# Spreading the maxima of k over the partitions: a transpose of the broadcast column in place of a float32 matrix product

## The chip, the core and the metric

The kernel runs on one core of a Trainium2 chip. Its time is device microseconds (us) of one launch; the clock starts and ends outside the span that the profiler shows, so a run's time is a little longer than its span. Five engines work side by side, each through its own queue in order: PE (TensorE; its weight loads are listed as PEld), ACT (ScalarE), DVE (VectorE), POOL (GpSimd, all but unused here) and SP (SyncE, which issues the transfers). An instruction waits at the head of its engine's queue until the semaphores that it names are there, and all that stands behind it on that engine waits too.

## The reference

Softmax attention without a sequence-by-sequence product, then two two-layer networks over the 4608 rows.

```python
def _attn_ref(q, k, v):                       # (8, 8, 576, 64): batch, heads, sequence, head width
    q_s = np.exp(q - np.max(q, axis=-1, keepdims=True))
    q_s = q_s / (np.sum(q_s, axis=-1, keepdims=True) + 1e-09)
    k_s = np.exp(k - np.max(k, axis=2, keepdims=True))      # maximum over the sequence
    k_s = k_s / (np.sum(k_s, axis=2, keepdims=True) + 1e-09)
    kv = np.einsum('bhsd,bhse->bhde', k_s, v)
    return np.einsum('bhsd,bhde->bhse', q_s, kv)

def _moe_ref(x, w_in, w_out):                 # 512 -> 2048 -> 512
    r = np.maximum(x @ w_in, 0.0)
    return (r * r) @ w_out

def _moe2_ref(x, w_gate, w_val, w_out):       # 512 -> 1536 -> 512
    gate = 1.0 / (1.0 + np.exp(-(x @ w_gate)))
    return (gate * (x @ w_val)) @ w_out
```

The change is in the third line of the attention: the maximum of k over the sequence, one number for each of the 64 columns of a head, has to be taken from every row of k, and rows lie on partitions.

## The kernel before, in words

Float32 products are made of three products of a high and a low part (`mm3`, L219 to L221), which is nearly all that PE does. The 4608 rows are nine blocks j of 512. Blocks 0 to 2 go through the first network by plain products (`c_in` and `c_out`; their middle results are `g0hl`); the later blocks go in pairs through seven products of half-size matrices instead of eight (`PRODUCTS`; their operands are `bX` for the first layer and `bS` for the second). Weights are split once and written to device memory; later they come back by `w_fetch` (L320) as tiles `ws`. Banks `bank0` to `bank5` of PSUM take the sums. At the end of block 2, `c_ev` copies `bank0` to `bank3` out: ACT copies two (L213, `x<-bank`), DVE the two others (L942, `x<-bank`), and SP stores the four (L947).

Attention for later blocks runs in the gaps. For a batch b and a pair of head pairs p (16 times in all) `plan_k` lays down this chain:

- DVE: `k_max` (L461, L464), the maximum of the sequence pieces, `kmx`;
- PE: `k_turn` (L470), two transposes of `kmx` into the PSUM tile `kps` (for b = 0 into a bank);
- DVE: `k_col` (L475), the maximum along the free axis, a column `km` of one number for each partition;
- PE: `k_all` (L483), which spreads that column over all partitions; this is what changes;
- DVE: `k_sub` (L488), k minus its maxima; ACT: `k_exp` (L492); PE: `k_mm` (L504), the products with v; DVE: `k_rec` (L512, L513); ACT: `k_copy` (L522).

For a block j and a pair p `plan_q` lays down a similar one: for j from 2 on DVE reduces (L565), PE swaps halves (`q_swap`, L575), DVE subtracts (L585, L586), ACT takes exp (L590), DVE sums (L565), PE swaps again (L575), DVE divides (L604 to L615) and transposes (L621), and PE multiplies by kv (L641).

The order of all of this isn't written out by hand. `Plan` holds each step with a due time, the cost that it is thought to have on its engine, the steps that it comes after and the buffers that it takes and gives. `Plan.trace` plays the steps through with these costs and records each when the engine comes free in that play:

```python
                    fn(*[e if a is CHOSEN else a for a in args])
                    us = engines[e]
                    busy[e] = now + us
```

So a cost in the table doesn't only describe a step: it decides what stands before what on every queue. The steps of the k chain touched here stand in `plan_k` (L666); the step of `k_all` is named "kgm" and has the cost 0.46 (1.1 for b = 0) on PE.

Of the kernel before, what the change touches and what calls it, by code (L numbers as in the profile page):

```python
# [23 lines left out]
DMA, PE, ACT, DVE, POOL, FREE = "DMA PE ACT DVE POOL FREE".split()  # L24
# [5 lines left out]
class Plan:  # L30
# [13 lines left out]
    def add(self, key, engines, name, fn, *args, after=(), take=(), give=(), slack=0.0):  # L44
        n = len(self.ops)
        assert name not in self.names, name
        self.names[name] = n
        self.ops.append((key, n, engines, name, fn, args, tuple(after), tuple(take), tuple(give), slack))
# [94 lines left out]
def attention_mlp_mlp(  # L143
# [20 lines left out]
    nc = tc.nc  # L164
# [24 lines left out]
    ident = cst.tile([128, 128], F32, name="ident")  # L189
# [6 lines left out]
    add = plan.add  # L196
# [281 lines left out]
    def k_all(b, p):  # L478

        m1, ps = kmx.pop((b, p)), kps[b, p]  # L480
        for n in range(2):
            at = slice(2 * C + C * n, 3 * C + C * n)
            nc.tensor.matmul(ps[:, at], m1[:, n:n + 1].to_broadcast([128, 128]), ident, start=True, stop=True)  # L483

    def k_sub(b, p):
        kt = kt_t[b, p].rearrange("p n (r c) -> p n r c", c=C)
# [177 lines left out]
    slack = lambda j: SLACK if j > 4 else 0.0  # L664

    def plan_k(b, p, key, step, wait=()):  # L666
        n = (b, p)
        vs = [(b, 2 * p + x) for x in range(2)]
        bank = [] if b == 0 else ["pa"]
        if b:  # L670
            add(key - 5, {DMA: 3.7}, ("kt",) + n, kv_load, b, p, after=wait, take=["k", "k"])
        else:
            add(p, {DMA: 1.84}, ("kt",) + n, k_load, b, p, take=["k"])
        for x in vs:
            if not b:
                add(p + 4, {DMA: 1.15}, ("vt",) + x, v_load, *x, take=["W"])
            add(key + 2.5 * step, {ACT: 0.22}, ("vo",) + x, v_ones, *x, after=[("kt",) + n if b else ("vt",) + x])
        for r in range(RK - 1):
            add(
                key + 0.1 * r, {DVE: 0.35}, ("km",) + n + (r,), k_max, b, p, r,  # L680
                after=[("km",) + n + (r - 1,) if r else ("kt",) + n], take=[] if r else ["km"],
            )
        add(key + 0.5 * step, {PE: 0.25 if b else 0.6}, ("kt2",) + n, k_turn, b, p, after=[("km",) + n + (RK - 2,)], take=bank, slack=slack(b))
        add(key + step, {DVE: 0.35}, ("kdg",) + n, k_col, b, p, after=[("kt2",) + n])
        add(key + 1.5 * step, {PE: 0.46 if b else 1.1}, ("kgm",) + n, k_all, b, p, after=[("kdg",) + n], give=["km"], slack=slack(b))
        add(key + 2 * step, {DVE: 1.4}, ("ks",) + n, k_sub, b, p, after=[("kgm",) + n], give=bank)
        add(key + 3 * step, {ACT: 1.15}, ("ke",) + n, k_exp, b, p, after=[("ks",) + n])
        add(
            key + 4 * step, {PE: 1.22 if b else 2.3}, ("kp",) + n, k_mm, b, p, after=[("ke",) + n] + [("vo",) + x for x in vs],
            take=bank, give=["k"] + (["k"] if b else ["W", "W"]), slack=slack(b),  # L690
        )
        add(key + 5 * step, {DVE: 0.36}, ("kr",) + n, k_rec, b, p, after=[("kp",) + n], take=["kr"])
        add(
            key + 6 * step, {ACT: 1.3}, ("kv",) + n, k_copy, b, p,
            after=[("kr",) + n] + (kv_users[b - 2, p] or [("kv", b - 2, p)] if b > 1 else []), give=["kr"] + bank,
        )
# [348 lines left out]
    for p in range(NP // 2):  # L1045
        plan_k(0, p, 3.37 * p, 0.86)
        plan_q(0, p, 3.37 * p + 3.62, 0.41)
# [67 lines left out]
    def plan_blocks(js, t, per):  # L1115

        for j in js:
            new = [b for _, b in segs(j) if b not in done_b]
            done_b.update(new)
            for p in range(NP // 2):  # L1120
                for b in new:
                    plan_k(b, p, t, 0.82, x_before.get(j, []))
                plan_q(j, p, t + 3.26, 0.58)
                t += 2 * per / NP
# [363 lines left out]
```

## Time and profile before

| | us |
|---|---|
| median of 3 runs | 1609.53 (1608.44 to 1611.57) |
| the profiled execution | 1610.02 |
| its span | 1608.2 |
| PE busy | 1577.2, 98% of the span |
| DVE busy | 1226.5, 76% |
| ACT busy | 940.2, 58% |
| waits of PE from 112 us on | 0.9 |

The span is what the profiler shows from the first to the last instruction. PE is busy almost all of it; a matmul row's end is modelled, and neighbours overlap, so that the pace of PE is read from the starts of rows that follow each other, not from a row's duration. The page's view of transfers and its groups name tiles by the program's names: `kps` and `km` are the tiles of the k chain, `qsw` and `qst` those of the q chain, `whl` and `wf` weights that are being split, `ws` weights fetched back.

### The profile page before, as it was taken

The numbers are of one execution on the slowest core, as the hardware profiler recorded it, in microseconds if no ns is written. First come the engines' busy times: TensorE is split into PE (matmuls) and PEld (weight loads), VectorE is DVE, ScalarE is ACT, GpSimd is POOL, SyncE is SP. The second block draws the span as 40 slices with busy tenths as digits, with TensorE's granted clock in tenths as the row PEclk, the third lists the DMA queues.
The fourth block names the chain that finished last, engine by engine and source line by source line (L and its number), as shares of the span: only waits on it lengthen the run. The fifth ranks groups of instructions, "written<-read, shape, count | busy, mean of one in ns | idle before, by whom it ended". The sixth has DMA issues, their size and how long they took to land.

```text
span 1608.2 us, 23070 instructions
## 1 busy us (share of the span) xinstructions
PE 1577.2 (98%) x8028; PEld 1301.7 (81%) x8028; DVE 1226.5 (76%) x2105; ACT 940.2 (58%) x1711; POOL 0.7 (0%) x6
## 2 busy tenths in 40 slices
PE   5899999999999999999999999999999999999998
PEld 3678888788878878888888888888888888888898
DVE  8988785899989999987977796448834784458547
ACT  6877655668686958785854564335523552335344
POOL 0000000000000000000000000000000000000000
PEclk9999999999999999999999999999999999999999
DMA  8987999998999989899989998656875677555896
GB/s 278 303 311 262 352 344 349 354 322 338 344 350 314 334 289 337 290 356 295 316 278 377 314 335 253 217 191 229 268 235 195 208 233 245 191 195 192 252 406 237
DMA packets 206835, 462.03 MB, mean 287 GB/s; under 512 B 78976, under 2 KB 78976, under 8 KB 206720
## 3 DMA queue, kind: packets, MB, share of 16 engines
q1 hardware_dynamic: 206720, 460.56, 82.8%
q8 instruction: 64, 1.05, 0.3%
q14 instruction: 51, 0.42, 0.1%
HBM read 364.54 MB, written 95.94 MB: 286 GB/s over the span
## 4 chain that ended last, share of the span: by engine, by line
PE 93%; DMA 2%; DVE 2%; ACT 1%; SPq 1%; issue 0%; DVEq 0%; ACTq 0%
PE bank L219 30%; PE bank L220 30%; PE bank L221 30%; PE xps L641 1%; PE kps L504 1%; DMA wraw<-in_moe_w_in_dram 1%; DMA vt<-in_v_dram 0%; DMA kt<-in_k_dram 0%; DMA w_in<-whl 0%; DMA wraw<-in_moe_w_out_dram 0%; DVE whl L216 0%; PE kps L483 0%; DVE wf L297 0%; SPq L250 0%; PE qsw L575 0%
## 5 line engine op out<-in xcount | busy, mean ns | idle before, releaser
L219 PE MATMUL bank<-bX,ws 128*128 128x512 f32 (+1 forms) x1176 | 442.3, 376 | 0.1
L221 PE MATMUL bank<-bX,ws 128*128 128x512 f32 (+1 forms) x1176 | 440.0, 374 | 0.0
L220 PE MATMUL bank<-bX,ws 128*128 128x512 f32 (+1 forms) x1176 | 439.8, 374 | 0.0
L821 DVE TENSOR_TENSOR s<-s,bank 128x512 f32<-128x512 f32 (+1 forms) x315 | 202.9, 652 | 197.2 <-PE bank L221 169.1
L213 ACT ACTIVATE s<-bank 128x512 f32<-128x512 f32 (+1 forms) x315 | 178.1, 572 | 189.8 <-PE bank L221 185.5
L219 PE MATMUL bank<-bS,ws 128*128 128x512 f32 (+1 forms) x756 | 287.2, 380 | 0.7 <-ACT s L213 0.7
L220 PE MATMUL bank<-bS,ws 128*128 128x512 f32 (+1 forms) x756 | 285.4, 378 | 0.0
L221 PE MATMUL bank<-bS,ws 128*128 128x512 f32 (+1 forms) x756 | 285.3, 377 | 0.0
L213 ACT ACTIVATE bS<-s 128x512 fp32r<-128x512 f32 (+1 forms) x330 | 195.2, 601 | 118.7 <-PE bank L221 94.4
L219 PEld LDWEIGHTS bank<-bX,ws 128*128 128x128 f32 x1176 | 221.4, 188 | 41.3 <-issue 1.3
L221 PEld LDWEIGHTS bank<-bX,ws 128*128 128x128 f32 x1176 | 221.4, 188 | 39.7
L220 PEld LDWEIGHTS bank<-bX,ws 128*128 128x128 f32 x1176 | 221.5, 188 | 39.0
L216 DVE TENSOR_TENSOR bS<-s,bS 128x512 fp32r<-128x512 f32 (+1 forms) x330 | 211.1, 649 | 32.5 <-ACT bS L213 32.0
L219 PEld LDWEIGHTS bank<-bS,ws 128*128 128x128 f32 x756 | 142.3, 188 | 28.4 <-ACT s L213 1.5
L221 PEld LDWEIGHTS bank<-bS,ws 128*128 128x128 f32 x756 | 142.2, 188 | 26.4
L220 PEld LDWEIGHTS bank<-bS,ws 128*128 128x128 f32 x756 | 142.3, 188 | 25.9 <-DVE bS L216 0.4
L840 ACT ACTIVATE s<-s 128x512 f32<-128x512 f32 (+1 forms) x120 | 70.6, 589 | 154.0 <-DVE s L821 153.5
L760 DVE TENSOR_TENSOR s<-s,s 128x512 f32<-128x512 f32 (+1 forms) x192 | 122.0, 650 | 1.1
L216 DVE TENSOR_TENSOR whl<-wf,whl 128x512 fp32r<-128x512 f32 x127 | 85.8, 685 | 19.1 <-ACT whl L213 18.6
L213 ACT ACTIVATE whl<-wf 128x512 fp32r<-128x512 f32 x127 | 78.4, 625 | 34.1 <-DVE wf L311 11.5
L267 ACT ACTIVATE wf<-wraw 128x512 f32<-128x512 f32 x68 | 44.9, 663 | 29.2 <-DMA wraw<-in_moe_w_out_dram 24.3
L219 PE MATMUL bank<-x,whl 128*128 128x512 f32 x128 | 54.1, 423 | 4.8 <-ACT x L213 3.8
(115 smaller groups left out, 1896.3 us busy)
## 6 DMA issues: line engine op xcount, KB each, us to landing
ws<-w_out SPq DMA_DIRECT2D x221, 512.0 KB, 5.1
ws<-w_gv SPq DMA_DIRECT2D x210, 512.0 KB, 4.4
ws<-w_in SPq DMA_DIRECT2D x100, 512.0 KB, 5.8
w_out<-whl SPq DMA_DIRECT2D x53, 512.0 KB, 5.8
w_gv<-whl SPq DMA_DIRECT2D x42, 512.0 KB, 5.0
w_in<-whl SPq DMA_DIRECT2D x32, 512.0 KB, 6.1
kt<-in_k_dram SPq DMA_DIRECT2D x16, 640.0 KB, 6.2
x2r<-x SPq DMA_DIRECT2D x36, 256.0 KB, 5.0
```

What stands on the lines that cost most here:

```text
L213: nc.scalar.activation(out=dst, in_=src, func=AF.Copy)
L216: by_name[engine].tensor_tensor(out=dst, in0=src, in1=hi.bitcast(F32), op=ALU.subtract)
L219: nc.tensor.matmul(ps, ah, bh, start=first, stop=False, skip_group_check=True)
L220: nc.tensor.matmul(ps, ah, bl, start=False, stop=False, skip_group_check=True)
L221: nc.tensor.matmul(ps, al, bh, start=False, stop=last, skip_group_check=True)
L267: nc.scalar.activation(out=t, in_=high.bitcast(F32), func=AF.Abs)
L504: nc.tensor.matmul(ps[D * g:D * g + D, o:o + D + 1], kt[:, n, C * r + D * h:C * r + D * h + D], vt[:, c:c + D + 1], start=(r == 0), stop=( ...
L641: nc.tensor.matmul(ps[a][col:col + D, e], kvf[b % 2][2 * p + n][row], t[n][row, e], start=True, stop=True, skip_group_check=True)
L760: by_name[engine].tensor_tensor(out=t[o], in0=t[a], in1=t[b], op=ALU.subtract)
L821: nc.vector.tensor_tensor(out=t, in0=t, in1=banks[pr[b]][:, 0:n], op=ALU.add)
L840: nc.scalar.activation(out=t, in_=t, func=AF.Sigmoid)
```

## The change

`k_all` calls PE's transpose in place of a matrix product with the identity. Both have the broadcast column as one operand and the identity as the other, and both leave the same numbers in the same place. The cost of the step in the plan's table is lowered to that of `k_turn`.

```diff
@@ def k_all(b, p) @@
         for n in range(2):
             at = slice(2 * C + C * n, 3 * C + C * n)
-            nc.tensor.matmul(ps[:, at], m1[:, n:n + 1].to_broadcast([128, 128]), ident, start=True, stop=True)
+            nc.tensor.transpose(ps[:, at], m1[:, n:n + 1].to_broadcast([128, 128]), ident)
@@ def plan_k @@
-        add(key + 1.5 * step, {PE: 0.46 if b else 1.1}, ("kgm",) + n, k_all, b, p, after=[("kdg",) + n], give=["km"], slack=slack(b))
+        add(key + 1.5 * step, {PE: 0.25 if b else 0.6}, ("kgm",) + n, k_all, b, p, after=[("kdg",) + n], give=["km"], slack=slack(b))
```

The second line moves instructions on PE, DVE, ACT and SP in the first half of the program. The largest move is around the place where block 2 ends (the last `g0hl` products into `bank3`, number 1164 of PE's L219 to L221) and the first pair of later blocks begins.

PE, from the 11th `k_turn` of the program (batch 5, p = 0) to its `k_mm`, before. Lines of "..." stand for `mm3` products; the two L575 belong to two different q tiles:

```order
L470 MATMUL kps_3354<-ident_78,kmx_3260 128x128 x2
...
L483 MATMUL kps_3354<-ident_78,km1_3371 128x128 x2
...
L221 MATMUL bank3_92<-g0hl_3249,ws_3207 128x512
L575 MATMUL qsw_3404<-qst_3327,swap_80 128x32
L575 MATMUL qsw_3406<-qst_3374,swap_80 128x32
L219 MATMUL bank4_93<-bX_3143,ws_3376 128x512
...
L504 MATMUL kps_3457<-vt_3148,kt_3146 64x65 x20
```

PE at the same place now. The two L575 are the two swaps of one q tile (`qst_3348` and `qst_3400` are its maxima and its sums):

```order
L221 MATMUL bank3_92<-g0hl_3207,ws_3150 128x512
L575 MATMUL qsw_3368<-qst_3348,swap_80 128x32
L470 MATMUL kps_3380<-ident_78,kmx_3342 128x128 x2
L483 MATMUL kps_3380<-ident_78,km1_3389 128x128 x2
L575 MATMUL qsw_3411<-qst_3400,swap_80 128x32
L504 MATMUL kps_3424<-vt_3220,kt_3218 64x65 x20
L219 MATMUL bank0_89<-bX_3213,ws_3407 128x512
```

The 12 `mm3` products that stood between `k_turn` and `k_all`, and the 30 between `k_all` and `k_mm`, now stand elsewhere: the steps of one k chain and one q chain follow each other with nothing in between, ahead of the next stage's first product.

DVE at this place, before: `k_sub` (L488) stands ahead of the two copies out of the banks (L942).

```order
L475 TENSOR_REDUCE km1_3371<-kps_3354 128x2
L216 TENSOR_TENSOR whl_3351<-wf_3308,whl_3351 128x512
L565 TENSOR_REDUCE qst_3374<-qt_3287 128x32
L488 TENSOR_TENSOR kt_3146<-kt_3146,kps_3354 128x2x640
L277 TENSOR_SCALAR wf_3394<-wf_3394 128x512
L283 TENSOR_SCALAR wf_3394<-wf_3394 128x512
L290 SCALAR_TENSOR_TENSOR wf_3394<-wraw_3348,wf_3394 128x512
L942 COPY x2_3418<-bank1_90 128x512
L297 ISA wf_3394<-wraw_3348,wf_3394 128x1024
L942 COPY x2_3423<-bank3_92 128x512
```

DVE now, with the last of the copies first:

```order
L942 COPY x2_3378<-bank3_92 128x512
L585 TENSOR_TENSOR qst_3348<-qst_3348,qsw_3368 128x32
L586 TENSOR_TENSOR qt_3254<-qt_3254,qst_3348 128x1024
L475 TENSOR_REDUCE km1_3389<-kps_3380 128x2
L311 TENSOR_TENSOR wf_3081<-wf_3081,wf_3077 128x512
L216 TENSOR_TENSOR whl_3346<-wf_3189,whl_3346 128x512
L565 TENSOR_REDUCE qst_3400<-qt_3254 128x32
L488 TENSOR_TENSOR kt_3218<-kt_3218,kps_3380 128x2x640
```

The copies of the banks have moved ahead of the k chain's two DVE steps, and the subtraction of q, a weight's sum and split and the sum over q stand between them.

SP at this place, before: the fetches of the next stage's weights (L320) stand ahead of the stores of block 2 (L947).

```order
L257 DMA wraw_3348<-in_moe2_w_gate_dram 128x512
L320 DMA ws_3369<-w_in05_2521 128x1024
L320 DMA ws_3376<-w_in06_2603 128x1024
L320 DMA ws_3380<-w_in02_366 128x1024
L257 DMA wraw_3398<-in_moe2_w_val_dram 128x512
L315 DMA w_in37_3410<-whl_3315 128x1024
L320 DMA ws_3425<-w_in07_2566 128x1024
L947 DMA x2_2_0_3445<-x2_3408 128x512
```

SP now:

```order
L947 DMA x2_2_0_3385<-x2_3370 128x512
L947 DMA x2_2_1_3387<-x2_3372 128x512
L947 DMA x2_2_2_3393<-x2_3376 128x512
L947 DMA x2_2_3_3398<-x2_3378 128x512
L257 DMA wraw_3404<-in_moe2_w_gate_dram 128x512
L320 DMA ws_3407<-w_in05_2591 128x1024
L320 DMA ws_3414<-w_in06_2632 128x1024
```

The four stores, which wait for the copies, have moved ahead of the fetch of `ws_3407`, the weights of the first product behind L504 on PE.

## Rows read from the trace of the kernel before

**Rows 1.** The page: busy us, share of the span and instructions of each engine.

```profile
PE 1577.2 (98%) x8028; PEld 1301.7 (81%) x8028; DVE 1226.5 (76%) x2105; ACT 940.2 (58%) x1711; POOL 0.7 (0%) x6
```

**Rows 2.** Waits of PE after 112 us: total us, times, longest.

```profile
PE bank L219 <- ACT s L213: 0.7, 1, 0.7
PE kps L470 <- DVE kmx L464: 0.2, 1, 0.2
```

**Rows 3.** PE groups by form, later batches: busy us, mean ns, idle before.

```profile
L483 PE MATMUL kps<-ident,km 128*128 128x128 f32 x56 | 8.5, 274 | 0.0
L470 PE MATMUL kps<-ident,kmx 128*128 128x128 f32 x28 | 5.5, 278 | 2.0 <-DVE kmx L464 1.7 <-ACT qf L213 0.3
```

**Rows 4.** Timeline of PE, 131 to 136 us: start us, us, instructions.

```profile
131.86 0.39 PE L221 MATMUL bank<-x,whl 128*128 128x512 f32 x1
132.09 0.38 PE L470 MATMUL kps<-ident,kmx 128*128 128x128 f32 x2
...
132.54 0.39 PE L220 MATMUL bank<-x,whl 128*128 128x512 f32 x1
...
134.83 0.39 PE L221 MATMUL bank<-x,whl 128*128 128x512 f32 x1
135.06 0.61 PE L483 MATMUL kps<-ident,km 128*128 128x128 f32 x4
...
135.74 0.39 PE L220 MATMUL bank<-x,whl 128*128 128x512 f32 x1
```

**Rows 5.** Timeline of PE where block 2 ends, 340 to 350 us.

```profile
340.14 0.61 PE L483 MATMUL kps<-ident,km 128*128 128x128 f32 x4
...
343.11 0.39 PE L221 MATMUL bank<-g0hl,ws 128*128 128x512 f32 x1
343.34 0.53 PE L575 MATMUL qsw<-qst,swap 128*128 128x32 f32 x4
343.70 0.48 PE L219 MATMUL bank<-bX,ws 128*128 128x512 f32 x1
...
348.00 1.39 PE L504 MATMUL kps<-vt,kt 128*64 128x65 f32 x40
349.32 0.50 PE L219 MATMUL bank<-bX,ws 128*128 128x512 f32 x1
```

**Rows 6.** Timeline of DVE at the same place, 337 to 347 us.

```profile
337.94 0.42 DVE L475 TENSOR_REDUCE km<-kps 128x2 f32<-128x256 f32 x1
...
338.87 1.21 DVE L565 TENSOR_REDUCE qst<-qt 128x32 f32<-128x1024 f32 x1
340.78 1.49 DVE L488 TENSOR_TENSOR kt<-kt,kps 128x1280 f32<-128x1280 f32 x1 [0.69 <-PE kps L483]
...
344.91 0.68 DVE L942 COPY x<-bank 128x512 f32<-128x512 f32 x1
345.51 0.17 DVE L585 TENSOR_TENSOR qst<-qst,qsw 128x32 f32<-128x32 f32 x1
345.72 1.23 DVE L586 TENSOR_TENSOR qt<-qt,qst 128x1024 f32<-128x1024 f32 x1
346.86 0.69 DVE L216 TENSOR_TENSOR whl<-wf,whl 128x512 fp32r<-128x512 f32 x1
```

**Rows 7.** Timeline of ACT at the same place: the exponential of k.

```profile
342.30 1.28 ACT L492 ACTIVATE kt<-kt 128x1280 f32<-128x1280 f32 x1 [3.42 <-DVE kt L488]
```

**Rows 8.** Timeline of SP's queue at the same place: fetches of weights, stores.

```profile
335.10 2.60 SPq L320 DMA_DIRECT2D ws<-w_in x3
...
344.08 2.27 SPq L947 DMA_DIRECT2D x<-x  x4
```

**Rows 9.** The page: issues of the fetch from w_in, KB each, us to landing.

```profile
ws<-w_in SPq DMA_DIRECT2D x100, 512.0 KB, 5.8
```

**Rows 10.** Timeline of PE: the first product, with the wait before it.

```profile
30.77 0.79 PE L219 MATMUL bank<-x,whl 128*128 128x512 f32 x1 [2.59 <-ACT x L213]
```

**Rows 11.** Busy time by stretch: us, then PE, PEld, DVE, ACT, POOL, granted clock, DMA, GB/s.

```profile
31.00:32.00 1.00, 1.00 (x2) 0.49 (x3) 1.00 (x2) 0.97 (x2) 0.00 (x0) 0.50 0.97 310
37.00:38.00 1.00, 1.00 (x6) 0.82 (x5) 1.00 (x3) 0.37 (x1) 0.00 (x0) 0.91 1.00 291
```

## The prediction

> **What bounds the kernel now.** I read the page's busy line first: PE 1577.2 of 1608.2 us [rows 1], so all that other engines could win is the 31.0 us in which PE stands. The waits of PE say where those lie: after 112 us only 0.9 us in two waits [rows 2]; the rest is the start-up, where PE waits for k, q and split weights, and the tail behind the last product. From 112 us on, then, PE sets the end: every instruction that it loses shortens the kernel by its slot, and every wait that it gains lengthens it, with no later slack to give it back. The reader should keep one thing in mind from that: PE takes its products in the order of the program, so a wait at the head of its queue also holds products whose operands are ready.
>
> **Part 1, the step itself.** The group of `k_all` has 56 instructions for 14 calls, four a call, that of `k_turn` 28, two a call [rows 3]: a float32 product is two instructions, a transpose one. Both rows show about 275 ns, but that is length, not pace. Pace comes from starts. Across two products and a `k_turn`, from L221 at 131.86 to L220 at 132.54, pass 0.68 us; across two products and a `k_all`, 134.83 to 135.74, pass 0.91 us [rows 4]; the two products alone are 2 x 0.23 (343.11 to 343.34 [rows 5]). So `k_turn` takes 0.22 us of PE, `k_all` 0.45, and as a transpose it should take what `k_turn` takes: 0.23 us less a call. Fourteen calls give 3.2 us, if PE is the bound at each; the first of them fall in the start-up, where a part goes into the next wait. I take twelve calls, -2.8 us, between -3.2 and -2.3 (ten).
>
> The Trainium skill, page "TensorE: Matmul & The Clock Gate", section "Part 4: PE-mode transpose", gives a 128 x 128 transpose about 275 ns in a kernel. As a price that would make the new `k_all` 0.55 us, dearer than the product's 0.45. The trace agrees with the figure as a length [rows 3] and not as a price: behind two transposes the next product comes after 0.22 us in all [rows 4].
>
> **Part 2, the order.** The lower cost in the table moves instructions, above all where block 2 ends. Before, PE has 12 products between `k_turn` and `k_all`, and 30 between `k_all` and `k_mm` (L483 at 340.14, L504 at 348.00 [rows 5]): 7.9 us in which DVE and ACT do their steps unseen. Now L575, L470, L483, L575, L504 follow each other with no product between them, and the next stage's `bX` products are queued behind. I follow the chain from T, the start of the first L575. Rows of DVE overlap by about 0.09 us (L586 is 1.23 long, and the next row starts 1.14 later [rows 6]); I use the pace.
>
> - The last `g0hl` product was issued 0.23 us before T and is 0.39 long [rows 5], so its copy L942 starts at about T+0.2 and takes 0.60: T+0.8 [rows 6].
> - L585 0.21, L586 1.14: T+2.15. They need the first L575, long done.
> - L475 0.34: T+2.5. PE now runs `k_all`.
> - On DVE stand L311 and L216 (0.60 each, as L942 on tiles of that size) and L565 (1.13) before `k_sub`: T+4.8. L488 would be ready to start at about T+3.0, but DVE is in order.
> - From L488 (340.78 [rows 6]) to the start of L492 (342.30 [rows 7]) pass 1.52 us: T+6.35.
> - L492 takes 1.28 [rows 7]: L504 starts at T+7.6.
>
> In these 7.6 us PE has two L575 (0.36 for two [rows 5]), L470 and the new L483 (0.22 each): 0.8 us of work. So PE stands for 6.8 us that it didn't stand for before, and all that waits on PE waits along. Bounds: without the rows in between (DVE's 2.3 us) the chain can't get below 4.5; if DVE, which has some 35 instructions to do between the last product of attention ahead of T and T itself (96 products of 0.23 us, 22 us), or the loads of k and q that it waits for are up to 1.5 us late, it is 8.3.
>
> A second chain says the same on another queue. The fetch of `ws_3407`, weights of the first product behind L504, now stands behind the four stores, the last of which waits for L942 (T+0.8). Four stores take 2.27 us of SP's queue [rows 8]; by T+2 the fetch is issued, and it lands 5.8 us later [rows 9], at T+7.8. Before, three such fetches were out at 335.10, eight us ahead of the place [rows 8]. L504 lasts until T+8.9 (1.32 from 348.00 to 349.32 [rows 5]), which covers the fetch; but a shorter k chain alone would not free PE.
>
> **Part 3, the clock.** At 30.77 us PE resumes after 2.59 us without work [rows 10]; from 31 us the granted clock reads 0.50, its lower level of 1.2 GHz, and it is back only between 37 and 38 us (0.91 there) [rows 11]. That is some 6.3 us at half pace, worth 3.2 us. The new wait is longer and has little work in it, in three pieces of 2 to 2.7 us; I expect the same fall. Part of the slow time will lie inside the wait, where it costs nothing. I take +2.5 us, between 0 and 3.2.
>
> **Part 4, the start-up.** The two calls of batch 0 and the first later ones feed PE when it waits anyway. In batch 1 `k_all` now comes right behind the q transposes, three products earlier than before, which should save some tenths; the order of DVE and ACT around it is dealt anew. PE's wait there is about 25 us in all (31.0 less 0.9 and a tail of about 5), most of it for the first loads, which the change doesn't touch. I take -0.5 us, between -1.5 and +1.5. Elsewhere on PE the chains keep their distance: the two swaps of a q tile stand at least 24 products apart, as before, and `k_turn` to `k_mm` at least 15.
>
> **The sum.** -2.8 + 6.8 + 2.5 - 0.5 = +6.0 us. The profiled execution took 1610.0 us, 0.5 above the median of 1609.5; on the median that gives 1615.5 us. About 0.2%, 3.2 us, is what a measurement of this kernel can tell from no change.
>
> **Rivals.**
>
> - *The step's gain alone* (faster). The chain at T is no wait in fact, since something I can't see gives PE work there. For it: in the order before PE lost only 0.9 us to waits after 112 us [rows 2], though other engines wait for PE there all the time. Against it: L504 needs L492, which needs L488, which needs L483 on the same PE, and no product lies between; that is order, not estimate. -2.8 - 0.5: 1606.2 us. It decides if the wait at L504 is under 1 us. Chance 0.09.
> - *The wait, but the clock stays up.* For it: PE does four small pieces of work in the wait. 1609.5 - 2.8 + 6.8 - 0.5 = 1613.0 us. Chance 0.25.
> - *A longer wait.* DVE reaches L942 late, because splits, sums and `bX` are dealt anew ahead of it, or the k load is late. +1.5 to +4 on the forecast: 1617 to 1619.5 us. Chance 0.17.
> - *A transpose that costs more than the product* (the change doesn't do what it says). 0.10 us more a call in place of 0.23 less: +1.4 in place of -2.8, 1619.7 us. Against it: the pace behind `k_turn` [rows 4]. The skill's section above names such a price. Chance 0.03.
>
> The forecast itself has 0.46.
>
> **How the numbers follow.** Slower by over 0.2% means above 1612.7: the forecast nearly whole (0.43), about half of the clock rival (0.13), the longer wait and the dear transpose (0.20): 0.76. Within 0.2%: the rest of the clock rival and of the forecast, with a little of the first rival, 0.17. Faster: 0.07. The range leaves out the first rival below and the far end of the longer wait above: from 1610.5 (a wait of 5.5, no fall of the clock, -1.5 at the start) to 1619.0.
>
> **What would show it.** Right: the waits of PE get a new group, L504 for ACT's L492, of 2 to 3 us, and L483 and the second L575 for DVE, together nearly 7 us, all near 340 us; the window behind it reads a clock of 0.50; `k_all` shows 28 instructions in place of 56, and PE's busy time falls by about 3 us in itself, before what the lower clock adds. Wrong: PE busy across that place as before, or a new wait elsewhere that is larger, in the start-up or at a fetch of `ws`. If the time is right and the wait at L504 is for a DMA instead, the second chain was the bound.

## The result, and the profile after

The changed kernel takes 1622.08 us (median of 6, 1619.88 to 1623.14) beside 1610.95 for the kernel before in the same rounds: ratio 1.0070, 95% interval 1.0057 to 1.0082. It is slower by some 11 us where the prediction had 6 and a range up to 9.5. The profiled execution has a span of 1619.6 us, 11.4 more than before. The page's busy line, to be read against [rows 1]:

```profile
PE 1576.1 (97%) x7996; PEld 1298.7 (80%) x7996; DVE 1222.2 (75%) x2102; ACT 944.1 (58%) x1717; POOL 0.7 (0%) x6
```

PE's instructions fell by 32, two for each of 16 calls, and its busy time by only 1.1 us. So the 11.4 us are time in which PE stands, or runs at the lower clock. The waits of PE after 112 us (total us, times, longest), beside [rows 2]:

```profile
PE kps L483 <- DVE km L475: 2.9, 1, 2.9
PE kps L504 <- ACT kt L492: 2.1, 1, 2.1
PE bank L219 <- ACT s L213: 1.9, 3, 0.7
PE qsw L575 <- DVE qst L565: 1.9, 1, 1.9
```

Three of the four groups lie at one place, where block 2 ends. PE's timeline there, beside [rows 5]; T is 344.81:

```profile
344.81 0.30 PE L575 MATMUL qsw<-qst,swap 128*128 128x32 f32 x2
344.94 0.41 PE L470 MATMUL kps<-ident,kmx 128*128 128x128 f32 x2
348.31 0.43 PE L483 MATMUL kps<-ident,km 128*128 128x128 f32 x2 [2.95 <-DVE km L475]
350.63 0.64 PE L575 MATMUL qsw<-qst,swap 128*128 128x32 f32 x2 [1.90 <-DVE qst L565]
353.33 2.44 PE L504 MATMUL kps<-vt,kt 128*64 128x65 f32 x40 [2.06 <-ACT kt L492]
355.69 0.79 PE L219 MATMUL bank<-bX,ws 128*128 128x512 f32 x1
356.29 0.43 PE L220 MATMUL bank<-bX,ws 128*128 128x512 f32 x1
```

These waits are 6.91 us. DVE's timeline at the place, beside [rows 6]:

```profile
345.28 1.28 DVE L942 COPY x<-bank 128x512 f32<-128x512 f32 x2
346.48 0.17 DVE L585 TENSOR_TENSOR qst<-qst,qsw 128x32 f32<-128x32 f32 x1
346.69 1.23 DVE L586 TENSOR_TENSOR qt<-qt,qst 128x1024 f32<-128x1024 f32 x1
347.83 0.42 DVE L475 TENSOR_REDUCE km<-kps 128x2 f32<-128x256 f32 x1
...
350.50 1.48 DVE L488 TENSOR_TENSOR kt<-kt,kps 128x1280 f32<-128x1280 f32 x1
```

It is the forecast chain, step for step, each some 0.9 us later against T than worked out: L475 at T+3.0 in place of 2.15, L488 at T+5.7 in place of 4.8, L504 at T+8.5 in place of 7.6. The reader finds the cause in the first row: two copies L942 stand there, not one, the second costing 0.60 us more, and the first starts at T+0.47 in place of T+0.2. SP's queue, beside [rows 8]:

```profile
345.82 2.58 SPq L947 DMA_DIRECT2D x<-x  x4
348.50 0.58 SPq L257 DMA_DIRECT2D wraw<-in_moe_w_gate_dram  x1
349.13 1.61 SPq L320 DMA_DIRECT2D ws<-w_in  x3
```

The fetch of `ws` is issued at T+4.3, behind the stores and a load that the prediction hadn't counted, in place of T+2. And the granted clock (the column before the DMA share), read from busy time by stretch in the same columns as [rows 11]:

```profile
348.00:350.00 2.00, 0.43 (x2) 0.19 (x2) 2.00 (x4) 1.52 (x2) 0.00 (x0) 0.88 1.04 382
350.00:352.00 2.00, 0.64 (x2) 0.50 (x2) 2.00 (x3) 0.00 (x0) 0.00 (x0) 0.50 0.99 298
354.00:356.00 2.00, 2.00 (x35) 1.88 (x32) 2.00 (x3) 0.42 (x1) 0.00 (x0) 0.50 1.01 414
356.00:358.00 2.00, 2.00 (x9) 1.60 (x9) 1.97 (x7) 0.82 (x3) 0.00 (x0) 0.91 1.03 422
```

The clock falls to its lower level (0.50, 1.2 GHz) as forecast. By these rows it is low from some 349.5 to 356.3 us, and of these 6.8 us nearly half, 3.2 us, lies inside the waits for `qst` and `kt`, where it costs nothing.

The place explains less than the whole. A second reading finds the rest. I number PE's L219, L220 and L221 products as they come in its timeline, and compare in two kernels the start of the product with one number: PE has then done the same main work. As the reference serves the profile of the first experiment below, the transpose with the order of before (span 1605.2). Microseconds later than there:

| kernel | product 168 | 408 | 1128 | 1272 | end of span |
|---|---|---|---|---|---|
| before | 0.0 | 0.5 | 1.2 | 1.5 | 3.0 |
| changed | 3.6 | 4.4 | 3.4 | 11.9 | 14.4 |
| e2, product, new figures | 5.6 | 6.9 | 6.6 | 15.1 | 20.5 |
| e13, 0.44 and 1.05 | -1.4 | -0.5 | -0.5 | -0.5 | -0.9 |
| e12, 0.48 and 1.15 | 7.4 | 6.0 | 7.6 | 7.2 | 8.4 |
| e3, new figure from batch 1 on | -1.1 | -0.3 | 4.8 | 14.4 | 16.4 |
| e4, new figure in batch 0 | 4.9 | 5.7 | 12.0 | 13.6 | 16.7 |
| e7, new figure from batch 3 on | 0.0 | 1.5 | 2.9 | 15.5 | 17.0 |
| e5, waits filled, first try | 1.4 | 3.4 | 3.7 | 13.6 | 16.0 |
| e10, waits filled | 1.9 | 3.0 | 2.0 | 9.5 | 12.3 |
| e8, L504 further back | 1.6 | 2.6 | 1.6 | 12.4 | 18.1 |
| e11, k chain further ahead | 1.8 | 3.5 | 2.8 | 17.5 | 19.4 |
| e9, order of before, start-up filled | 2.1 | 2.0 | 2.0 | 2.0 | 1.9 |

The e rows are kernels of the experiments below. Block 2 ends at product 1164: 1128 lies 36 products (8 us) ahead of the place, 1272 lies 108 behind it. In the row of the changed kernel the start-up loses 3.4 us, the place 8.5, and the rest of the kernel 2.5. (As the orders differ, a product's number doesn't fix how much attention work PE has behind it: at 408 the changed kernel has 16 products L641 more behind it than e1, some 1.1 us, which are not a loss; at 1128 all counts agree.) Of the last part, 1.8 us arise at two places, products 3096 (819 us) and 3819 to 3822 (984 us), and 1.2 of these are two more waits of L219 for ACT's `s` than the one of before; 0.6 us arise ahead of them, and I can't place those. The orders still differ at both places: those of ACT, DVE and SP become equal to those of before only at some 1000 to 1026 us, later than "the first half of the program" that the section on the change names.

The start-up, in PE's waits from 24 to 112 us of the changed kernel:

```profile
PE bank L219 <- ACT x L213: 5.8, 2, 4.0
PE bank L219 <- ACT g L914: 2.8, 3, 1.8
PE bank L504 <- ACT kt L492: 1.8, 1, 1.8
PE qps L627 <- issue: 1.5, 2, 1.3
```

The same view of before has 3.8, 1.0, 1.9 and 0.2 in these groups: PE now waits longer for ACT, for its results of the first layer (`g`) and its copies (`x`). The longest, 4.0 us, is ahead of the first product and is no loss, since that product still starts 0.9 us earlier than in e1 (30.88 beside 31.73 us). The one that costs most is at product 96. PE's row there in the changed kernel, the row of before, and a stretch behind it in the changed kernel:

```profile
73.38 0.79 PE L219 MATMUL bank<-x,whl 128*128 128x512 f32 x1 [1.83 <-ACT x L213]
72.45 0.49 PE L219 MATMUL bank<-x,whl 128*128 128x512 f32 x1 [1.26 <-ACT x L213]
76.00:78.00 2.00, 2.00 (x6) 1.61 (x5) 2.00 (x6) 0.32 (x2) 0.00 (x0) 0.50 0.94 290
```

Behind the wait of 1.83 us the granted clock is 0.50 until nearly 80 us; behind the wait of 1.26 us before it stayed at 1.00. The clock takes more than the wait: against e1 the changed kernel is 0.9 us late at product 96 (73.38 beside 72.52 us) and 3.2 at product 112 (80.31 beside 77.08), so 2.4 us of the start-up's loss are PE's products at the lower clock. ACT's copies of `x` start 0.9 us later there than in e1 (72.73 beside 71.87 us), since a step ahead of them on ACT's queue waited 0.98 us for a load.

### The profile page after: what moved, and what is told of

Same layout as the page of the kernel before. It is cut to its first block, busy times and chain, and to the rows that moved or that the text cites. A ratio compares the mean times of both kernels' runs of the same rounds, so it can differ in the third digit from the quotient of the medians.

```text
span 1619.6 us, 23003 instructions
## 1 busy us (share of the span) xinstructions
PE 1576.1 (97%) x7996; PEld 1298.7 (80%) x7996; DVE 1222.2 (75%) x2102; ACT 944.1 (58%) x1717; POOL 0.7 (0%) x6
## 3 DMA queue, kind: packets, MB, share of 16 engines
q8 instruction: 64, 1.05, 0.3%
## 4 chain that ended last, share of the span: by engine, by line
PE 91%; DMA 3%; DVE 3%; ACT 1%; issue 1%; SPq 0%; DVEq 0%; ACTq 0%
PE bank L219 30%; PE bank L220 29%; PE bank L221 29%; PE kps L504 1%; DMA vt<-in_v_dram 1%; PE xps L641 1%; DMA qt<-in_q_dram 1%; DMA wraw<-in_moe_w_in_dram 1%; DVE bX L216 1%; DMA w_in<-wf 0%; DMA w_out<-whl 0%; ACT qt L597 0%; DVE qst L565 0%; DVE kt L488 0%; DVE xf L760 0%
## 5 line engine op out<-in xcount | busy, mean ns | idle before, releaser
L219 PE MATMUL bank<-bX,ws 128*128 128x512 f32 (+1 forms) x1176 | 441.9, 376 | 0.1
L221 PE MATMUL bank<-bX,ws 128*128 128x512 f32 (+1 forms) x1176 | 439.9, 374 | 0.0
L220 PE MATMUL bank<-bX,ws 128*128 128x512 f32 (+1 forms) x1176 | 439.8, 374 | 0.0
L219 PE MATMUL bank<-bS,ws 128*128 128x512 f32 (+1 forms) x756 | 287.7, 381 | 1.9 <-ACT s L213 1.9
L220 PE MATMUL bank<-bS,ws 128*128 128x512 f32 (+1 forms) x756 | 285.5, 378 | 0.0
L221 PE MATMUL bank<-bS,ws 128*128 128x512 f32 (+1 forms) x756 | 285.4, 377 | 0.0
L219 PEld LDWEIGHTS bank<-bX,ws 128*128 128x128 f32 x1176 | 221.5, 188 | 41.1 <-issue 0.8
L221 PEld LDWEIGHTS bank<-bX,ws 128*128 128x128 f32 x1176 | 221.5, 188 | 39.8
L220 PEld LDWEIGHTS bank<-bX,ws 128*128 128x128 f32 x1176 | 221.6, 188 | 38.9
L219 PEld LDWEIGHTS bank<-bS,ws 128*128 128x128 f32 x756 | 142.3, 188 | 30.5 <-ACT s L213 3.5
L221 PEld LDWEIGHTS bank<-bS,ws 128*128 128x128 f32 x756 | 142.2, 188 | 26.5
L220 PEld LDWEIGHTS bank<-bS,ws 128*128 128x128 f32 x756 | 142.3, 188 | 25.8 <-DVE bS L216 0.4
L216 DVE TENSOR_TENSOR whl<-wf,whl 128x512 fp32r<-128x512 f32 x127 | 85.7, 684 | 14.2 <-ACT whl L213 13.6
L219 PE MATMUL bank<-x,whl 128*128 128x512 f32 x128 | 54.5, 426 | 8.7 <-ACT x L213 5.8
L216 DVE TENSOR_TENSOR g0hl<-g,g0hl 128x512 fp32r<-128x512 f32 x48 | 32.7, 684 | 29.8 <-ACT g0hl L213 29.6
```

The costliest lines, as they stand in the source:

```text
L216: by_name[engine].tensor_tensor(out=dst, in0=src, in1=hi.bitcast(F32), op=ALU.subtract)
L219: nc.tensor.matmul(ps, ah, bh, start=first, stop=False, skip_group_check=True)
L220: nc.tensor.matmul(ps, ah, bl, start=False, stop=False, skip_group_check=True)
L221: nc.tensor.matmul(ps, al, bh, start=False, stop=last, skip_group_check=True)
```

## Experiments

Times of before in the same rounds were 1609.78 (e1 to e4), 1610.80 (e5 to e9), 1609.59 (e10, e11) and 1610.40 (e12, e13); all comparisons are of five rounds.

**e1: the step without its order.** The transpose stays, the figures of the table go back; every engine then has exactly the order of before.

```diff
-        add(key + 1.5 * step, {PE: 0.25 if b else 0.6}, ("kgm",) + n, k_all, ...
+        add(key + 1.5 * step, {PE: 0.46 if b else 1.1}, ("kgm",) + n, k_all, ...
```

> The transpose alone: the new step with the old figures in the table (0.46 and 1.1), so that every engine has the order of the kernel before. Theory A (the order costs, the step itself pays): 0.23 us less a call, 12 to 14 calls, 2.8 to 3.2 us: about 1608 us beside 1611, ratio near 0.998, the k_all group at 28 instructions, no new wait of PE. Rival T (a transpose is dearer than the product): about +1.4 us, 1612.4. Rival B (PE has slack at these places, the step is worth nothing): 1611.

Measured: 1605.87 us, ratio 0.9974 (0.9965 to 0.9984), by the ratio 4.2 us less, 2.6 to 5.6 by the interval; 3.0 us less in the spans. Theory A holds for the step. Followed from call to call, the row of before in the table grows by 0.24 us at each from the fifth on, and by nothing in the first four, whose gain goes into waits of the start-up; twelve calls of 0.24 are 2.9. PE's waits after 112 us are those of [rows 2] again, word for word:

```profile
PE bank L219 <- ACT s L213: 0.7, 1, 0.7
PE kps L470 <- DVE kmx L464: 0.2, 1, 0.2
```

and the group of `k_all` by form, beside [rows 3]:

```profile
L483 PE MATMUL kps<-ident,km 128*128 128x128 f32 x28 | 5.3, 272 | 0.0
```

The length of one is 272 ns beside 274 before; half the instructions are gone, and the group's busy time is 5.3 us beside 8.5. The Trainium skill gives about 275 ns for a 128 x 128 transpose in a kernel ("TensorE: Matmul & The Clock Gate", section "Part 4: PE-mode transpose"); this trace agrees with that as a length, and the 0.24 us a call show that it isn't what the queue pays: a call of two transposes takes 0.45 less 0.24, some 0.2 us.

**e2: the order without the step.** The matrix product stays, the new figures are in the table; the order is that of the changed kernel.

```diff
-        add(key + 1.5 * step, {PE: 0.46 if b else 1.1}, ("kgm",) + n, k_all, ...
+        add(key + 1.5 * step, {PE: 0.25 if b else 0.6}, ("kgm",) + n, k_all, ...
```

> The order alone: the float32 matrix product stays, the table has the new figures (0.25 and 0.6), so that every engine has the order of the changed kernel. Theory A: the waits of the changed kernel come back whole (L483, L575 and L504 together about 7 us near 345 us, and the loss ahead of it), and the 3 us of the step are missing: about 1625 us. Rival T: without the transpose the time is that of before, 1611.

Measured: 1626.39 us, ratio 1.0100 (1.0081 to 1.0118), theory A's 1625 within the interval. All of the loss is there without a single new transpose, and the three waits stand in PE's timeline as in the changed kernel:

```profile
351.48 0.71 PE L483 MATMUL kps<-ident,km 128*128 128x128 f32 x4 [2.94 <-DVE km L475]
353.81 0.64 PE L575 MATMUL qsw<-qst,swap 128*128 128x32 f32 x2 [1.62 <-DVE qst L565]
356.50 2.43 PE L504 MATMUL kps<-vt,kt 128*64 128x65 f32 x40 [2.06 <-ACT kt L492]
```

The pair e1 and e2 settles the main question: the line in `k_all` is worth about -3 to -4 us, the line in `plan_k` +16.6. (The two don't simply add: in the new order the step is worth 16.6 less 11.1, 5.5 us. By the table e2 is 3.2 us behind the changed kernel at product 1128, no more at 1272, and 6.1 at the end, and its profile has one more wait of L219 for `s`, 1.16 us at 924 us.) From here on the question is why the order costs so much.

**e13 and e12: other figures beside the old ones.** Is it this figure, or any new order?

```diff
-        add(key + 1.5 * step, {PE: 0.25 if b else 0.6}, ("kgm",) + n, k_all, ...
+        add(key + 1.5 * step, {PE: 0.44 if b else 1.05}, ("kgm",) + n, k_all, ...
```

> The transpose, with figures a little below the old ones (0.44 and 1.05). PE's order differs from the kernel before in some fifty places by a few products, that of DVE and ACT in the start-up more; the k steps stand where they stood, at 1140, 1152 and 1182 where block 2 ends. Theory A: as the transpose alone within 1 us, 1605 to 1607. Rival D: several us more.

That was e13; e12 goes to the other side of the old figures.

```diff
-        add(key + 1.5 * step, {PE: 0.25 if b else 0.6}, ("kgm",) + n, k_all, ...
+        add(key + 1.5 * step, {PE: 0.48 if b else 1.15}, ("kgm",) + n, k_all, ...
```

> The transpose, with figures in the table a little above the old ones (0.48 and 1.15). Every engine's order is dealt anew from the start-up on, but the k steps of the call where block 2 ends stand at 1128, 1152 and 1188 products and its two L575 at 1140 and 1188, so nothing piles up there. Theory A (what costs is the pile and the place where waits fall, not the sign of the figure's error): no run of waits near 345 us; the start-up loses 0 to 4 us against the transpose alone: 1606 to 1610. Rival D (the old order suits this kernel, and any other costs about as much as those tried so far): 1616 or more.

Measured: e13 1605.97 us, 0.9973 (0.9961 to 0.9985), as e1. e12 1615.58 us, 1.0035 (1.0023 to 1.0048). e12 lies between the two expectations. Nothing piles up where block 2 ends, and products 1128 to 1272 lose nothing, as theory A said; but the start-up alone loses 7.4 us by product 168, not 0 to 4. In e12's timeline of PE:

```profile
67.93 2.18 PE L504 MATMUL kps<-vt,kt 128*64 128x65 f32 x40 [4.17 <-ACT kt L492]
```

and by stretch, with a granted clock of 0.50 behind that wait:

```profile
70.00:72.00 2.00, 0.58 (x9) 0.35 (x6) 1.81 (x6) 1.47 (x6) 0.00 (x0) 0.50 0.85 220
```

L504 was put three products behind L483 there, some 0.7 us of work, and the k chain between them takes longer than that: PE waits 4.17 us.

**e3, e4 and e7: the new figure in one part of the kernel.** In the place of `0.25 if b else 0.6` e3 has

```diff
+        add(key + 1.5 * step, {PE: 0.25 if b else 1.1}, ("kgm",) + n, k_all, ...
```

> The transpose, with the new figure for the batches after the first only (0.25, and 1.1 for batch 0). The order has the same pile of k steps where block 2 ends as the changed kernel, but another start-up. Theory A (two places, the pile and the start-up): pile 6.9 us of wait and 1.6 of clock, less 3.2 of the step: about +5, 1616 us, with the start-up's own share open by 2 us. Rival S (all of the loss follows from the start-up): 1608. Rival P (all of it is the pile): 1622.

e4 has

```diff
+        add(key + 1.5 * step, {PE: 0.46 if b else 0.6}, ("kgm",) + n, k_all, ...
```

> The transpose, with the new figure for batch 0 only (0.46 and 0.6). The start-up has the order of the changed kernel up to 159 products behind the first k step, and the k steps near block 2's end have 12 and 42 products between them. Theory A: no wait of PE for L504 near 345 us; the start-up's loss of about 3.9 us stays, less 3.2 of the step: about 1611.7 us. Rival P (all of the loss is the pile): 1608. Rival S (all of it is the start-up): 1622.

and e7 has

```diff
+        add(key + 1.5 * step, {PE: (0.25 if b >= 3 else 0.46) if b else 1.1}, ("kgm",) + n, k_all, ...
```

> The transpose, with the new figure from batch 3 on only. The start-up has the order of before (positions of all k steps up to 318 products are the same), and the k steps of the call where block 2 ends stand at 1164 products together, as in the changed kernel. Theory A: start-up as in the kernel with the transpose alone, the pile as in the changed kernel (8.7 us between products 1104 and 1248): about 1606 + 9 = 1615, with 1 to 2 us open for the order in between. Rival S (the pile hurts only behind the changed start-up, which leaves DVE late): under 1611. Rival P (the start-up has no part in it): 1620 or more.

Measured: e3 1624.65 us, 1.0097 (1.0078 to 1.0117); e4 1621.92 us, 1.0070 (1.0052 to 1.0088); e7 1625.00 us, 1.0088 (1.0074 to 1.0102). None met theory A's number; the times are near those of rival P (e3, e7) and rival S (e4), but the table shows neither as the cause. e7 has the start-up of e1, e3 one of its own; both have the pile, as meant, and lose nothing by product 168; between 1128 and 1272 they lose 9.6 (e3) and 12.6 us (e7). So the pile needs no changed start-up, and what it costs isn't fixed: the steps in it wait for whatever DVE, ACT and SP have been dealt. e4 has no pile where block 2 ends, but its order put two steps of PE together 110 us earlier:

```profile
232.89 0.31 PE L575 MATMUL qsw<-qst,swap 128*128 128x32 f32 x2
237.15 0.41 PE L575 MATMUL qsw<-qst,swap 128*128 128x32 f32 x2 [3.95 <-DVE kt L488]
```

My mistake in these expectations was the same: I took a figure changed in one part to move only that part. The play in `Plan.trace` carries a shift on to the end.

**e5: work in the waits, first try.** Transposes of the identity in the three waits should keep the clock up, so that the rest of the waits' price shows alone.

```diff
+    fill = lambda ps, at, n: [nc.tensor.transpose(ps[:, at:at + 128], ident, ident) for _ in range(n)]
 def k_all(b, p):
+        fill(kps[b, p], 2 * C, 22 if (b, p) == (5, 0) else 0)
 def k_mm(b, p):
-        ps = kps[b, p] = k_bank(b, p)
+        ps = kps[b, p] = k_bank(b, p); fill(ps, 0, 15 if (b, p) == (5, 0) else 0)
```

14 more stand ahead of the second `q_swap` of (5, 0), in that swap's own tile.

> The changed kernel with transposes of the identity written into PE's queue in the three waits where block 2 ends (22 ahead of L483, 14 ahead of the second L575, 15 ahead of L504; 0.11 us of pace each, so 2.4, 1.5 and 1.7 us in waits of 2.95, 1.90 and 2.06). The order of everything else stays. Theory A: the waits remain (L504 still 8.5 us behind the first L575), the granted clock reads near 1.00 from 346 to 358 us, L504 lasts 1.39 in place of 2.44 us, the next products 0.40 in place of 0.79 and 0.43: 1 to 2 us less, 1620 to 1621 beside 1622. As the prediction sized it (clock 2.5 us): 1619.5. Rival (the clock lies wholly behind the fetch of ws): no change, 1622, and a new wait of L219 for the DMA of ws.

Measured: 1622.54 us, 1.0072 (1.0056 to 1.0089), no change; but it wasn't the test that it should be. PE's timeline:

```profile
348.60 4.16 PE L452 MATMUL kps<-ident 128*128 128x128 f32 x22 [2.94 <-DVE km L475]
352.60 0.38 PE L483 MATMUL kps<-ident,km 128*128 128x128 f32 x2
...
356.35 1.39 PE L504 MATMUL kps<-vt,kt 128*64 128x65 f32 x40
```

The added work writes the tile `kps` that DVE's L475 is still reading, so it waited behind L475 and lay on the path: L504 11.2 us behind the first L575 (345.11) in place of 8.5. Work put into a wait here needed a bank that nobody reads at that time.

**e10: the same in a free bank.** The bank of the second L575 is taken earlier, and 18 and 12 transposes write it; 9 stay ahead of L504.

```diff
 def k_all(b, p):
+        if (b, p) == (5, 0): early.append(pa.tile([128, N], F32, tag="pa", name="qsw")); fill(early[0], 128, 18)
```

> The changed kernel with transposes of the identity in PE's queue in the same three waits as in the run before that did so, but 18 and 12 of them now write the bank of the second L575, which no other engine reads at that time, and 9 that of L504: 2.0, 1.3 and 1.0 us of pace in waits of 2.95, 1.90 and 2.06. Theory A: L504 starts 8.3 to 8.5 us behind the first L575, as without them; the granted clock stays near 1.00; L504 lasts 1.39 in place of 2.44, L483 and L575 their short lengths, and the next products 0.40: 1.5 to 2 us less by then, the first bX product 9.2 us behind the first L575 in place of 10.9, 1620 to 1620.5 in all. If the fetch of ws is late behind it, a wait of L219 for a DMA takes a part of that, up to all. Rival (the bank isn't free either): the transposes start late and lie on the path, 1622 or more.

Measured: 1619.46 us, 1.0064 (1.0052 to 1.0076). PE's timeline, T at 343.38:

```profile
345.28 2.18 PE L452 MATMUL qsw<-ident 128*128 128x128 f32 x18 [1.34 <-DVE qst L585]
347.30 0.38 PE L483 MATMUL kps<-ident,km 128*128 128x128 f32 x2
...
351.90 1.39 PE L504 MATMUL kps<-vt,kt 128*64 128x65 f32 x40
353.61 0.50 PE L219 MATMUL bank<-bX,ws 128*128 128x512 f32 x1 [0.32 <-DMA ws<-w_in]
```

By stretch, the clock in the middle of it:

```profile
350.00:352.00 2.00, 1.30 (x11) 1.06 (x13) 1.97 (x5) 1.28 (x1) 0.00 (x0) 1.00 0.99 320
```

L504 starts at T+8.52, as in the changed kernel to the hundredth; the granted clock is 1.00 throughout, and L504 takes 1.39 in place of 2.44 us. From product 1128 to 1272 pass 44.3 us in place of 45.2: the clock's fall costs 1.0 us here, not 2.5 (one profile of each kernel; the place takes 8.5 us in e2 as well). The fetch of `ws`, for which the first `bX` product now waits until T+10.2, takes 0.3 us of what the clock could give. (The times say no more than that: beside before in the same rounds e10 takes 9.9 us more and the changed kernel 11.1; of the 2.1 us between the two spans 1.4 lie ahead of product 1128, where the two kernels have the same order.)

**e8 and e11: the k chain taken out of the place.** e8 gives its steps a longer slack, so that L504 comes 24 products later; e11 plans the call 18 us earlier, so that L470, L483 and L504 stand at products 1140, 1152 and 1164.

```diff
-        add(key + 1.5 * step, {PE: 0.25 if b else 0.6}, ("kgm",) + n, k_all, ..., slack=slack(b))
+        add(key + 1.5 * step, {PE: 0.25 if b else 0.6}, ("kgm",) + n, k_all, ..., slack=4.4 if (b, p) == (5, 0) else slack(b))
```

So in e8, with the same slack for `k_mm` and the second `q_swap` of (5, 0).

> The changed kernel with L504 of the call where block 2 ends 24 products further back (a longer slack for that call's steps in the table); the order of PE ahead of it is the same, behind it the table deals it anew. The prediction's second chain: PE then stands for the fetch of ws, which is issued behind the x stores and lands about 10 us behind the first L575, so the first bX product still starts near 355 us with a wait of about 4 us for a DMA: 1620 to 1622. Rival W (the k chain alone held PE): the bX products start near 351.5 us, and 2.1 us of wait and 1 us of clock go: about 1619 or less.

In e11:

```diff
-                    plan_k(b, p, t, 0.82, x_before.get(j, []))
+                    plan_k(b, p, t - (18 if (b, p) == (5, 0) else 0), 0.82, x_before.get(j, []))
```

> The changed kernel with the k call where block 2 ends planned 18 us earlier: L470, L483 and L504 of it stand at 1140, 1152 and 1164 products, with the start-up up to 1128 products unchanged; three L575 of q stand at 1164, and behind them the first bX products. It tells what is late next when the k chain is spread. Theory A: nearly no wait for L504; the q chain (L575, DVE's L585 and L586, ACT, DVE's L565, the second L575) and the fetch of ws behind the x stores still hold the bX products, so they start 8 to 10 us behind the last g0hl product, with a wait for DVE's qst of 4 us or more, or for the DMA of ws: 1618 to 1621. Rival W (the k chain alone is the wait): the 6.9 us of wait and 1.6 of clock go: 1613.

Measured: e8 1625.48 us, 1.0091 (1.0077 to 1.0104); e11 1626.15 us, 1.0102 (1.0089 to 1.0115). Without L504 there, PE still stands in both. In e8 the first `bX` product starts 10.6 us behind the first L575 (343.04), but not for a DMA, as I expected; a third L575, which the table now puts there, waits:

```profile
353.19 0.64 PE L575 MATMUL qsw<-qst,swap 128*128 128x32 f32 x2 [3.69 <-DVE kt L488]
353.64 0.78 PE L219 MATMUL bank<-bX,ws 128*128 128x512 f32 x1
```

What releases it by the profile is L488, a step of the k chain on DVE, so e8 alone doesn't exclude rival W. e11 does: there the k chain is spread, L504 waits 0.15 us, and everything else that is late shows, one behind the other:

```profile
344.95 1.39 PE L504 MATMUL kps<-vt,kt 128*64 128x65 f32 x40 [0.15 <-ACT kt L492]
346.26 0.41 PE L575 MATMUL qsw<-qst,swap 128*128 128x32 f32 x2
352.91 0.64 PE L575 MATMUL qsw<-qst,swap 128*128 128x32 f32 x2 [6.24 <-DVE qst L565]
354.73 0.61 PE L575 MATMUL qsw<-qst,swap 128*128 128x32 f32 x2 [1.18 <-DVE qst L604]
359.74 0.80 PE L219 MATMUL bank<-bX,ws 128*128 128x512 f32 x1 [4.39 <-DMA ws<-w_in]
```

The two waits for q hold PE for 7.4 us, and then the fetch for 4.4, since here two loads of k and v stand ahead of it on SP's queue. So the place has three chains of nearly one length: L504 starts 8.5 us behind the first L575 (changed kernel), the last of the swaps for q 8.5 us behind the first of them (e11), and the fetch has landed after 10.2 us (e10). The changed kernel's 8.5 us belong to none of them alone. That the chain in front of the new stage must have work of PE beside it, whichever chain it is, is what the order of before gets right.

**e9: work in the waits of the start-up,** with e1's order: 14 transposes ahead of the second L470, 18 ahead of the second L504, 8 ahead of the first product.

```diff
 def k_mm(b, p):
-        ps = kps[b, p] = k_bank(b, p)
+        ps = kps[b, p] = k_bank(b, p); fill(ps, 0, 18 if (b, p) == (0, 1) else 0)
```

> The transpose with the old figures (the order of before), and transposes of the identity in three waits of the start-up (14 ahead of the second L470, 18 ahead of the second L504, 8 ahead of the first product of the first stage). Theory A (a wait of PE costs again behind it, by the lower clock): the granted clock stays near 1.00 from 17 to 36 us, the two L504 last 1.39 in place of 2.44 us, the first products of the stage 0.40 in place of 0.63 to 0.79: 2 to 4 us less than the transpose alone, about 1603. Rival (the start-up waits for loads, DVE and ACT, so a faster PE only waits longer): 1606.

Measured: 1607.56 us, 0.9984 (0.9975 to 0.9992): no better than e1, whose interval overlaps with this one, and not 3 us ahead. In PE's timeline the 18 wait for DVE, run at half pace and delay L504 from 26.74 (e1) to 27.99:

```profile
24.21 3.85 PE L452 MATMUL bank<-ident 128*128 128x128 f32 x18 [2.61 <-DVE kt L488]
27.99 1.39 PE L504 MATMUL bank<-vt,kt 128*64 128x65 f32 x40
...
44.64 0.66 PE L627 MATMUL qps<-ident,qt 128*128 128x128 f32 x4 [1.84 <-ACT qf L213]
```

From 28 to 75 us the clock reads 1.00, and the products of the first stage run at full pace (0.40 us in place of 0.63 to 0.79); two waits that e1 doesn't have, of 1.18 us at 41.26 and of 1.84 us for ACT, take that back. So in this stretch a faster PE waits longer, as the rival said; the late L504 blurs the rest. At product 96 e9 waits 1.65 us, and the clock reads 0.50 behind that too, from 76 to 78 us, though the order is that of before: it loses 1.6 us there and has them back by product 168.

## Why the prediction was off, point by point

- **Part 1, the step (-2.8): right.** -3.0 us between the spans of e1 and before, 0.24 us a call against 0.23 worked out, and twelve calls that count. The dear transpose is out.
- **Part 2, the wait (+6.8): right in mechanism; that the size fits is partly luck.** 6.91 us in three waits, all at the named place. But the chain ran 0.9 us late, since DVE has two copies L942 where one of 0.60 us was counted, and starts the first at T+0.47 in place of T+0.2; and PE's own steps took 1.6 us in place of 0.8, since ahead of a wait a step takes its length (0.41 for L470, 0.43 for L483) and not its pace of 0.22, and the second L575 ran at the low clock (0.64 us). The two errors cancel in the wait. The second chain was right as a warning (e11), but mis-sized: the fetch is issued at T+4.3, not T+2, and landed near T+10.2 (e10), not T+7.8.
- **Part 3, the clock (+2.5): right that it falls, mis-sized.** 1.0 us (e10): of the 6.8 slow us, 3.2 lay in the waits, and the fetch covers another 0.3. Parts 2 and 3 together were 9.3 us forecast and 8.5 measured.
- **Part 4, the start-up (-0.5, at most +1.5): the step that failed.** Five profiles with this order of PE up to product 1128 (changed, e5, e8, e10, e11) lose 3.4, 3.7, 1.6, 2.0 and 2.8 us against e1. The prediction took `k_all` standing "three products earlier than before" as a gain of some tenths, named the new deal of DVE and ACT without a price, and didn't follow what ACT and DVE deliver, `g` and `x`, to the products behind. "Elsewhere on PE the chains keep their distance" was true and beside the point: the loss is L219 waiting for ACT and, behind such a wait, the lower clock, which the prediction looked for only where block 2 ends. In the changed kernel the stretch from product 96 to 112 loses 2.4 us by it; in the four others it loses 1.2 (e5), 0.4 (e8), 1.3 (e10) and 1.6 (e11), in the kernel before nothing. So a part of the 3.4 is what this one profile met. Which change of order makes ACT late isn't shown, beyond the one load named above.
- **What the sum left out: the rest of the kernel.** 2.5 us behind product 1272, of which 1.8 arise where L219 waits for ACT's `s`, at 819 and 984 us. The prediction put nothing there, since the chains on PE keep their distance; the orders of ACT, DVE and SP weren't followed that far. e5 and e10 lose 2.4 and 2.8 us there too.

Measured in the prediction's own terms: -3.0 + 8.5 + 3.4 + 2.5 = +11.4 us. The forecast's +6.0 is right in its first three terms to a microsecond (6.5 beside 5.5), partly because their errors offset each other, and misses 6.4 in the others. No rival reached 1622: "a longer wait" ended at 1619.5, and the dear transpose, at 1619.7 the nearest, is excluded by e1. A new deal costs also away from the place that one can point to; that belonged into the range, upwards. (The lower end of the range adds up to 1610.7 by its own terms, not 1610.5.)

What stays open: why six other orders that the plan deals (e3, e4, e7, e8, e11, e12) all lose 8.4 to 19.4 us against that of before, where e13's, which differs little, loses nothing. The figure of 0.25 us is nearer to the 0.22 us that the step takes than 0.46, and yet deals the worse order; no run here tells whether the old figures are merely a lucky draw.

The version that beats both is the smallest: the transpose with the table untouched (e1, 0.9974; e13 is the same within the interval).

## What to carry to other kernels

Where a table of costs sets the order, change the step and its cost in two kernels, not in one: here the step gives 3 us and the truer cost takes away 14. When such an order moves, go through every engine that feeds the bound one and look for places where its queue has no work between two steps of one chain; and put a price on the start-up that can go up as well as down, since it is dealt anew too.

## What the runs showed of the hardware

- Transposes alone hold the granted clock, and bring it back. In e10 PE had nothing but transposes, one swap and L483, with three gaps of 1.3, 0.2 and 1.0 us, between 343.9 and 351.9 us, and the clock read 1.00 in every stretch; in the changed kernel, with the same waits left empty, it read 0.50 from 350 us. In e5 PE ran nothing but 22 transposes from 348.60 to 352.60 us, and the clock read 0.55 from 350 to 352 and 1.00 from 352 to 354; these 22 took 4.16 us (0.19 each) and the 14 behind them 1.69 (0.12 each). e9 shows the same: 0.52 from 26 to 28 us, with transposes alone since 24.21, and 1.00 from 28. The Trainium skill says in "Part 4: PE-mode transpose" of "TensorE: Matmul & The Clock Gate" that the full clock doesn't engage for transpose mode; for these float32 transposes the trace says otherwise, and the trace decides.
- Waits of nearly one length end differently. In the changed kernel product 96 came at 73.38 us, after 1.83 us without work, and ran at 0.50 from its start (0.79 us long); in e2, with the same order, it came at 74.39 us after 1.85 us, was 0.51 us long at 1.00, and the clock fell only behind it, to 0.53 from 76 to 78 us, and was back earlier. That wait cost 2.4 us by product 112 in the changed kernel and 1.3 in e2. Five profiles of one order differ by up to 2 us at product 1128.
